# Threshold attention and an MLP on one core: ten blocks by products of quarters instead of eight, and the division of x^T moved to other engines

## The chip, the core and the metric

The kernel runs on one core of a Trainium2 chip. The core has five engines that run side by side, each through its own list of instructions in order: TensorE (PE, with its weight loads as PEld) multiplies matrices, VectorE (DVE) and ScalarE (ACT) work element by element, GpSimd (POOL) does the same more freely and issues transfers, and SyncE (SP) issues transfers. TensorE writes to PSUM, a small memory of banks; everything else is in SBUF. The metric is the time of one execution in microseconds on the device. The kernel before takes 1418.27 us, the median of three runs (1416.62 to 1419.5).

## The reference

q, k and v have 8 batches, 8 heads, 576 rows and 64 columns. They come in single precision, the weights w_in (512 x 2048) and w_out (2048 x 512) as doubles.

```
scores = scale * q @ k^T                         # per head, 576 x 576
thresh = max(scores, axis=-1) - tau
scores = where(scores >= thresh, scores, -1e9)
attn   = exp(scores - max(scores)) / (sum + 1e-09)
x      = attn @ v, the heads side by side        # 4608 x 512
h      = x @ w_in                                # 4608 x 2048
g      = 0.5 * h * (1 + erf(h / sqrt(2)))        # exact Gelu
out    = g @ w_out                               # 4608 x 512
```

## The kernel before

**Pairs, chunks and slots.** Two heads of a batch form a pair; there are 32 pairs, four to a batch. The 576 rows of a pair are worked on in five chunks: chunks 0 to 3 have 128 rows of each head, and chunk 4 has the last 64 rows of both heads together. A chunk is a slot of the main loop (L824), and the document names slots of a pair by the chunk, 0 to 4. The first four pairs (batch 0) are the early ones: their slots come in another order (two chunks of each pair, then three of each), since during them the weights are loaded and converted as well. The early part has 20 slots, the rest 140.

**A slot.** TensorE forms the scores of the chunk in two PSUM tiles, one a head (`scores`, L358; one tile in chunk 4). There are only two such tiles, so the scores of the next slot wait for the end of this slot's softmax. VectorE takes the negated maximum of each (`nmx`, L370), GpSimd derives the threshold (`thr`, L371), ScalarE the exponential (L373), VectorE multiplies it by the comparison with the threshold and sums (L389), and, beyond the early pairs, transposes the result in squares of 32 (`turn_p`, L436). SP moves the squares to their places in `pT` (`regroup`, L454, L458). In slot 2 of the next pair, `weigh_v` (L460) multiplies pT by V into two PSUM tiles of x^T. The softmax isn't divided by its sums before that; `divisors` (L405), in slot 4, takes the reciprocals and sends them through DRAM into a row on all partitions, `inv`. After `weigh_v`, VectorE multiplies x^T by `inv` out of PSUM into the block `x_blk` in SBUF (L492), in pieces that end at blocks of 256 tokens. For the early pairs the division is made earlier, and ScalarE copies x^T (L490).

**The MLP.** Tokens are taken in 18 blocks of 256. `block_steps` (L538) gives a plain block: 64 matmuls of 256 columns into hT (L549), Gelu by ScalarE (L522), and 32 matmuls of 512 columns into o_ps (L563), a copy and a store. ScalarE has the Gelu and the exponential in different tables; `table` (L532) brings the exponential's back with a dummy. In the early part hT is only copied, and its Gelus wait in a list, `held`, until slot 20. `fill` issues matmuls of plain blocks between the scores of one slot and the next. How many it issues is a plan written by hand: `GOAL` says how many blocks are to be done by which slot, `goal` draws lines between, and `PARTS` spreads a pair's share over its five slots. The plan doesn't look at the time that anything takes. `tokens` says up to which token the blocks may be taken.

**Products of quarters.** The last 8 blocks (`PLAIN = N_BLK - 8`) aren't worked on during the attention. They wait as x in SBUF, three of them (`AWAY`) in DRAM (`put_away`, `bring`), and `strassen` (L654) does them two at a time, a duo, with seven products of quarters instead of eight in both layers, at the price of sums on VectorE. `weights_in` (L612) forms the sums of w_in after the last chunk.

**The start.** `load_early` brings q and k of an early pair: q by SP's queue, k by ScalarE's for pairs 0 and 1, else by SP's. `load_piece` brings a piece of the weights twice, as it is and shifted by a byte (L156, L158), on GpSimd's queue, and `convert` lets VectorE and ScalarE turn pieces to single precision (L178 to L188) for a given number of nanoseconds in each slot. GpSimd clears `q_tail` and `v_sb` first of all, and tau is the first thing on SP's queue.

Of the kernel before, what the change touches and what calls it, by code (L numbers as in the profile page):

```python
# [18 lines left out]
def kernel(  # L19
# [46 lines left out]
    TOK = 256  # L66
    N_BLK = B * S // TOK
    PLAIN = N_BLK - 8

    AWAY = [PLAIN, PLAIN + 1, PLAIN + 2]  # L70
    order = list(range(PLAIN + 3, N_BLK)) + AWAY
# [33 lines left out]
    for t in q_tail + v_sb:  # L105
        nc.gpsimd.memset(t, 0.0)
# [4 lines left out]
    tau_sb = const.tile([P, 1], FP32, name="tau_sb")  # L111
    nc.sync.dma_start(tau_sb, tau[0].partition_broadcast(P))
    some = const.tile([P, 1], FP32, name="some")
    nc.vector.tensor_scalar(some, tau_sb, 0.0, None, op0=ALU.is_ge)
    q_scale = const.tile([P, 1], FP32, name="q_scale")
    nc.vector.tensor_scalar(q_scale, some, SCALE, None, op0=ALU.mult)
    lift = const.tile([P, 1], FP32, name="lift")
    nc.vector.tensor_scalar(lift, some, -ALL, ALL, op0=ALU.mult, op1=ALU.add)
    tau_eff = const.tile([P, 1], FP32, name="tau_eff")
    nc.vector.tensor_scalar(tau_eff, tau_sb, lift, None, op0=ALU.max)  # L120
# [18 lines left out]
    def load_piece():  # L139
        if loaded[0] == len(pieces):  # L140
            return
        dst, src = pieces[loaded[0]]
        loaded[0] += 1
        if not wide:
            nc.sync.dma_start(dst, src)
            converted[0] += 1
            load_piece()
            return
        k = loaded[0] - 1
        if k % 2:  # L150

            room = pd[k // 2 % 2].bitcast(U32)
            raw, shifted = room[:, 0:2 * PIECE], room[:, 2 * PIECE:4 * PIECE]
        else:
            raw, shifted = (xg.tile([P, 2 * PIECE], U32, tag="x", name=s) for s in ("raw", "shifted"))
        nc.gpsimd.dma_start(raw, src.bitcast(U32))  # L156
        n = 8 * PIECE - 4
        nc.gpsimd.dma_start(shifted.bitcast(U8)[:, 0:n], src.bitcast(U8)[:, 3:3 + n])  # L158
        raws.append((dst, raw, shifted))
# [300 lines left out]
    def weigh_v(p, lo, hi):  # L460
# [34 lines left out]
        if by is not None:  # L495
            return divide
        divide()
# [289 lines left out]
    load_early(0)  # L787
    nc.scalar.activation(warm[:, 1:2], warm[:, 0:1], AF.Exp)
    load_early(1)
    for _ in range(2):  # L790
        load_piece()
# [25 lines left out]
    PARTS = 1.2, 1.2, 0.8, 1.2, 0.6  # L817
# [6 lines left out]
    for n in range(len(slots) + WEIGH + 1):  # L824
# [12 lines left out]
        made = []  # L837
# [3 lines left out]
        if p > EARLY and i == WEIGH:  # L841
            made = [weigh_v(p - 1, lo, hi) for lo, hi in ((0, WIDE), (WIDE, S))]
# [45 lines left out]
        convert(3000 if n < 2 * HP else 3650 if n < BATCH - 1 else 1e9)  # L888
# [15 lines left out]
        elif p > EARLY and i == WEIGH and p % HP == 0:  # L904
# [38 lines left out]
```

## Time and profile before

| what | value |
|---|---|
| median of three runs | 1418.27 us |
| the profiled execution | 1413.93 us |
| its span | 1412.1 us |
| early part, to the first maximum of slot 20 | 0 to 152.1 us |
| first matmul by quarters (chain) | 1019.11 us |
| VectorE: maxima L370, products L389, transposes L436 | 749, 816, 1376 ns each |
| ScalarE: exponential L373, table load L522, Gelu L522 | 738, 1283, 597 ns each |
| VectorE: multiplies of x^T, L492 | 104 of them, 31.7 us |
| GpSimd: thr L371 | 292 ns each |

The profile is of one execution, 0.3% below the median. A row of the page gives an engine's operation with its line, what it writes and reads, how often, its total and mean time, and the idle time before it. The granted clock of TensorE was 0.997 in this execution. TensorE's busy time takes modelled ends for its matmuls, so it says less than the times between starts. One float32 matmul shows as two records. In the timeline, one row can stand for several instructions of a group that follow each other, and its duration then reaches from the first start to the last end.

### The profile page before, as it was taken

The numbers are of one execution on the slowest core, as the hardware profiler recorded it, in microseconds if no ns is written. First come the engines' busy times: TensorE is split into PE (matmuls) and PEld (weight loads), VectorE is DVE, ScalarE is ACT, GpSimd is POOL, SyncE is SP. The second block draws the span as 40 slices with busy tenths as digits, with TensorE's granted clock in tenths as the row PEclk, the third lists the DMA queues.
The fourth block names the chain that finished last, engine by engine and source line by source line (L and its number), as shares of the span: only waits on it lengthen the run. The fifth ranks groups of instructions, "written<-read, shape, count | busy, mean of one in ns | idle before, by whom it ended". The sixth has DMA issues, their size and how long they took to land.

```text
span 1412.1 us, 19647 instructions
## 1 busy us (share of the span) xinstructions
PE 1377.0 (98%) x6544; PEld 956.6 (68%) x6544; DVE 886.8 (63%) x1772; ACT 636.3 (45%) x1052; POOL 389.0 (28%) x812
## 2 busy tenths in 40 slices
PE   6899899999999999999999999999999999999999
PEld 4677557466475564655746657466588888888887
DVE  5888687777777777777777777777664142241330
ACT  5766628445255373563745627447141140230320
POOL 4444244343344344344334344330000000000000
PEclk9999999999999999999999999999999999999999
DMA  9979267666666766666766776664400000001000
GB/s 259 294 276 261 68 140 154 134 150 127 141 150 135 162 131 140 143 146 150 164 132 145 164 158 143 148 140 100 108 1 8 23 1 26 19 1 51 9 8 23
DMA packets 219346, 167.05 MB, mean 118 GB/s; under 512 B 122480, under 2 KB 203952, under 8 KB 219248
## 3 DMA queue, kind: packets, MB, share of 16 engines
q1 hardware_dynamic: 193040, 108.65, 36.5%
q0 software_dynamic: 23808, 56.57, 13.1%
q8 instruction: 53, 0.87, 0.3%
q10 hardware_dynamic: 2400, 0.59, 0.2%
q14 instruction: 45, 0.37, 0.1%
HBM read 71.68 MB, written 11.47 MB: 59 GB/s over the span
## 4 chain that ended last, share of the span: by engine, by line
PE 91%; DVE 4%; ACT 3%; DMA 2%; issue 1%; SPq 0%; POOL 0%; DVEq 0%; ACTq 0%; POOLq 0%
PE bank L683 27%; PE hT L549 20%; PE o_ps L563 19%; PE sc L358 12%; PE xT L475 10%; PE tr L301 2%; DVE p L389 1%; ACT p L373 1%; DMA q<-in_q_dram 1%; DVE power L186 1%; DMA turned_p<-in_moe_w_in_dram 1%; DVE nmx L370 0%; DVE w_in L188 0%; ACT diag L403 0%; DVE power L178 0%
## 5 line engine op out<-in xcount | busy, mean ns | idle before, releaser
L373 ACT ACTIVATE p<-sc,nmx 128x576 f32<-128x576 f32 x288 | 202.1, 738 | 370.8 <-DVE nmx L370 370.6
L370 DVE TENSOR_REDUCE nmx<-sc 128x1 f32<-128x576 f32 x288 | 205.1, 749 | 163.1 <-PE sc L358 163.0
L563 PE MATMUL o_ps<-w_out,g 128*128 128x512 f32 x640 | 294.3, 602 | 3.0 <-ACT g L522 3.0
L549 PE MATMUL hT<-x,w_in 128*128 128x256 f32 x1280 | 296.1, 384 | 0.0
L549 PEld LDWEIGHTS hT<-x,w_in 128*128 128x128 f32 x1280 | 238.6, 190 | 56.0 <-issue 25.1
L389 DVE SCALAR_TENSOR_TENSOR p<-sc,thr,p 128x576 f32<-128x576 f32 x288 | 225.4, 816 | 65.1 <-ACT p L373 62.7
L371 POOL TENSOR_SCALAR thr<-nmx,tau_eff 128x1 f32<-128x1 f32 x288 | 84.1, 292 | 541.8 <-DVE nmx L370 541.8
L563 PEld LDWEIGHTS o_ps<-w_out,g 128*128 128x128 f32 x640 | 116.5, 190 | 142.6 <-issue 137.8
L358 PE MATMUL sc<-kT,qT 64*128 64x288 f32 x960 | 165.1, 437 | 1.4 <-DVE p L389 1.0
L475 PE MATMUL xT<-pT,v 128*64 128x256 f32 (+1 forms) x1280 | 163.7, 409 | 2.7 <-ACT g L522 2.7
L436 DVE STREAM_TRANSPOSE turned_p<-p 128x1152 f32<-128x1152 f32 x112 | 154.1, 1376 | 2.9
L358 PEld LDWEIGHTS sc<-kT,qT 64*128 64x128 f32 x960 | 93.4, 190 | 82.9 <-issue 70.3
L475 PEld LDWEIGHTS xT<-pT,v 128*64 128x64 f32 x1280 | 89.8, 137 | 74.0 <-issue 10.8
L233 POOL DMA_DIRECT2D v<-in_v_dram x208 | 110.5, 534 | 10.7 <-issue 9.8
L683 PE MATMUL bank<-x,w_in 128*128 128x256 f32 x384 | 93.3, 379 | 0.0
L683 PE MATMUL bank<-w_out,unit 128*128 128x256 f32 x416 | 92.4, 379 | 0.0
L522 ACT ACT_TABLE_LOAD x67 | 86.0, 1283 | 1.2
L535 ACT ACT_TABLE_LOAD x67 | 86.0, 1283 | 1.2
L683 PEld LDWEIGHTS bank<-w_out,unit 128*128 128x128 f32 x416 | 79.1, 190 | 10.7
L683 PEld LDWEIGHTS bank<-x,w_in 128*128 128x128 f32 x384 | 73.0, 190 | 10.3 <-issue 0.5
L224 POOL DMA_DIRECT2D q<-in_q_dram x104 | 70.7, 685 | 16.0 <-issue 15.1
L224 POOL DMA_DIRECT2D k<-in_k_dram x104 | 69.6, 675 | 0.7 <-DMA inv<-turned 0.3
(152 smaller groups left out, 1307.3 us busy)
## 6 DMA issues: line engine op xcount, KB each, us to landing
pT<-turned_p SPq DMA_DIRECT2D x448, 160.0 KB, 3.5
pT<-pd_tail SPq DMA_DIRECT2D x112, 80.0 KB, 2.9
q<-in_q_dram POOLq DMA_DIRECT2D x104, 72.0 KB, 4.1
k<-in_k_dram POOLq DMA_DIRECT2D x104, 72.0 KB, 2.6
inv<-turned SPq DMA_DIRECT2D x56, 128.0 KB, 3.9
v<-in_v_dram POOLq DMA_DIRECT2D x156, 40.0 KB, 3.2
out_dram<-o_sb SPq DMA_DIRECT2D x20, 256.0 KB, 4.3
raw<-in_moe_w_in_dram POOLq DMA_DIRECT2D x8, 512.0 KB, 5.6
```

What stands on the lines that cost most here:

```text
L224: eng.dma_start(t[e * D + f:e * D + f + Q], rows[:, :, f:f + Q])
L233: eng.dma_start(t[r:P:4, e, 0:n, :], rows[:, r * KR:r * KR + n, :])
L358: nc.tensor.matmul(sc[e][:, h, 0:HALF], lhsT=lhsT, rhs=s["kT"][rows, at:at + HALF], start=True, stop=True)
L370: nc.vector.tensor_reduce(nmx[:, e:e + 1], sc, axis=AXIS.XY, op=ALU.max, negate=True)
L373: nc.scalar.activation(w[:, e * S:(e + 1) * S].rearrange("p (h s) -> p h s", h=2), sc, AF.Exp, bias=nmx[:, e:e + 1], scale=1.0)
L389: nc.vector.scalar_tensor_tensor(row, sc[e][:, :, 0:HALF], thr[:, e:e + 1], row, op0=ALU.is_ge, op1=ALU.mult, accum_out=den[e])
L436: nc.vector.transpose(turned_p[:, :, i // 2, 0:NB, i % 2 * Q:(i % 2 + 1) * Q], w.rearrange("p (e b i) -> p e b i", e=2, i=Q))
L475: nc.tensor.matmul(to, lhsT=s["v"][:, e, c, :], rhs=rhs, start=(c == 0), stop=(c == KR - 1))
L522: nc.scalar.activation(t, src, AF.Gelu)
L549: nc.tensor.matmul(hT[:, j % 2, :], lhsT=w_in_sb[c][:, j * P:(j + 1) * P], rhs=x_blk[n][:, c, :], start=(c == 0), stop=(c == N_DM - 1))
L563: nc.tensor.matmul(o[:, 0:d_model], lhsT=g[j][:, m * P:(m + 1) * P], rhs=w_out_sb[j], start=(j == 0), stop=(j == N_DF - 1))
L683: nc.tensor.matmul(to, lhsT=l, rhs=r, start=start and k == 0, stop=k == len(pairs) - 1, skip_group_check=not start)
```

## The change

Four things are changed. Ten blocks instead of eight go by quarters (`PLAIN = N_BLK - 10`), five of them by way of DRAM. x^T beyond the early pairs is copied out of PSUM by ScalarE, as it was for the early ones, and multiplied by `inv` in SBUF by GpSimd, a pair at a time (`divide`), in slot 3 (`DIVIDE`), after that slot's thr; for the last pair in the slot of its weighing. A batch's tokens are let into the MLP one slot later. `GOAL` and `PARTS` have other numbers. At the start, k of pair 1 comes on GpSimd's queue ahead of the memsets, tau behind the q of pair 0, the first two pieces of weights on SP's queue; slot 0 has no conversion, and slots 1 to 7 have 3400 ns instead of 3000.

```diff
-    PLAIN = N_BLK - 8
-
-    AWAY = [PLAIN, PLAIN + 1, PLAIN + 2]
-    order = list(range(PLAIN + 3, N_BLK)) + AWAY
+    PLAIN = N_BLK - 10
+
+    AWAY = list(range(PLAIN, PLAIN + 5))
+    order = list(range(PLAIN + 5, N_BLK)) + AWAY
...
-    for t in q_tail + v_sb:
-        nc.gpsimd.memset(t, 0.0)
...
-    tau_sb = const.tile([P, 1], FP32, name="tau_sb")
-    nc.sync.dma_start(tau_sb, tau[0].partition_broadcast(P))
...
-    def load_piece():
+    def load_piece(eng=nc.gpsimd):
...
-        nc.gpsimd.dma_start(raw, src.bitcast(U32))
+        eng.dma_start(raw, src.bitcast(U32))
...
-        nc.gpsimd.dma_start(shifted.bitcast(U8)[:, 0:n], src.bitcast(U8)[:, 3:3 + n])
+        eng.dma_start(shifted.bitcast(U8)[:, 0:n], src.bitcast(U8)[:, 3:3 + n])
...
-            eng = nc.scalar if p < 2 and name == "k" else nc.sync
+            eng = (nc.scalar, nc.gpsimd)[p] if p < 2 and name == "k" else nc.sync
...
-        by = None if p < EARLY else s["inv"]
-        if hi == S:
-            del st[p]
-
-        def divide():
-            at = lo
-            while at < hi:
-                n, o = divmod(b * S + at, TOK)
-                size = min(TOK - o, hi - at)
-                if n not in x_blk:
-                    x_blk[n] = xg.tile([P, N_DM, TOK], FP32, tag="x", name="x")
-                to, x = x_blk[n][:, hp, o:o + size], xT[:, at - lo:at - lo + size]
-                if by is None:
-                    nc.scalar.copy(to, x)
-                else:
-                    nc.vector.tensor_tensor(to, x, by[:, at:at + size], op=ALU.mult)
-                at += size
...
+        for n, o, at, size in in_blocks(b, lo, hi):
+            if n not in x_blk:
+                x_blk[n] = xg.tile([P, N_DM, TOK], FP32, tag="x", name="x")
+            nc.scalar.copy(x_blk[n][:, hp, o:o + size], xT[:, at - lo:at - lo + size])
+
+    def in_blocks(b, lo, hi):
+        while lo < hi:
+            n, o = divmod(b * S + lo, TOK)
+            size = min(TOK - o, hi - lo)
+            yield n, o, lo, size
+            lo += size
+
+    def divide(p):
+        b, hp = divmod(p, HP)
+        by = st.pop(p)["inv"]
+        for n, o, at, size in in_blocks(b, 0, S):
+            x = x_blk[n][:, hp, o:o + size]
+            nc.gpsimd.tensor_tensor(x, x, by[:, at:at + size], op=ALU.mult)
...
     load_early(0)
+    tau_sb = const.tile([P, 1], FP32, name="tau_sb")
+    nc.sync.dma_start(tau_sb, tau[0].partition_broadcast(P))
...
     load_early(1)
+    for t in q_tail + v_sb:
+        nc.gpsimd.memset(t, 0.0)
     for _ in range(2):
-        load_piece()
+        load_piece(nc.sync)
...
+    DIVIDE = 3
...
-    GOAL = [(-1, 0.0), (START - 1, 0.0), (BATCH - 1, 0.5)]
-    GOAL += [(BATCH * (m + 2) + WEIGH, x) for m, x in enumerate([1.96, 3.3, 4.64, 5.98, 7.32, 8.66, PLAIN])]
+    GOAL = [(-1, 0.0), (START - 1, 0.0), (BATCH - 1, 0.42)]
+    GOAL += [(BATCH * (m + 2) + DIVIDE, x) for m, x in enumerate([1.96, 2.97, 3.98, 4.98, 5.99, 6.99])]
+    GOAL += [(BATCH * B + WEIGH, PLAIN)]
...
-    PARTS = 1.2, 1.2, 0.8, 1.2, 0.6
+    PARTS = 1.3, 1.3, 0.2, 1.3, 0.9
...
         if p > EARLY and i == WEIGH:
-            made = [weigh_v(p - 1, lo, hi) for lo, hi in ((0, WIDE), (WIDE, S))]
+            for lo, hi in (0, WIDE), (WIDE, S):
+                weigh_v(p - 1, lo, hi)
+            if p == NP:
+                divide(p - 1)
...
-        if made:
-            made[0]()
...
-        if made:
-            made[1]()
...
+        if EARLY < p < NP and i == DIVIDE:
+            divide(p - 1)
...
-        convert(3000 if n < 2 * HP else 3650 if n < BATCH - 1 else 1e9)
+        convert(0 if n == 0 else 3400 if n < 2 * HP else 3650 if n < BATCH - 1 else 1e9)
...
-        elif p > EARLY and i == WEIGH and p % HP == 0:
+        elif p > EARLY and i == DIVIDE and p % HP == 0 or p == NP and i == WEIGH:
             tokens = p // HP * S
```

More of the change, by code (lines that the diff above doesn't have):

```diff
@@ L104 @@
     pd_tail = [const.tile([P, 4 * KR, Q], FP32, name=f"pd_tail{i}") for i in range(2)]
-    for t in q_tail + v_sb:
-        nc.gpsimd.memset(t, 0.0)
-    tau_sb = const.tile([P, 1], FP32, name="tau_sb")
-    nc.sync.dma_start(tau_sb, tau[0].partition_broadcast(P))
-    some = const.tile([P, 1], FP32, name="some")
-    nc.vector.tensor_scalar(some, tau_sb, 0.0, None, op0=ALU.is_ge)
     q_scale = const.tile([P, 1], FP32, name="q_scale")
-    nc.vector.tensor_scalar(q_scale, some, SCALE, None, op0=ALU.mult)
-    lift = const.tile([P, 1], FP32, name="lift")
-    nc.vector.tensor_scalar(lift, some, -ALL, ALL, op0=ALU.mult, op1=ALU.add)
     tau_eff = const.tile([P, 1], FP32, name="tau_eff")
-    nc.vector.tensor_scalar(tau_eff, tau_sb, lift, None, op0=ALU.max)
     rebias = const.tile([P, 1], FP32, name="rebias")
@@ L476, in weigh_v @@
                     to, lhsT=s["v"][:, e, c, :], rhs=rhs, start=(c == 0), stop=(c == KR - 1))
-        by = None if p < EARLY else s["inv"]
-        if hi == S:
-            del st[p]
-        def divide():
-            at = lo
-            while at < hi:
-                n, o = divmod(b * S + at, TOK)
-                size = min(TOK - o, hi - at)
-                if n not in x_blk:
-                    x_blk[n] = xg.tile([P, N_DM, TOK], FP32, tag="x", name="x")
-                to, x = x_blk[n][:, hp, o:o + size], xT[:, at - lo:at - lo + size]
-                if by is None:
-                    nc.scalar.copy(to, x)
-                else:
-                    nc.vector.tensor_tensor(to, x, by[:, at:at + size], op=ALU.mult)
-                at += size
-        if by is not None:
-            return divide
-        divide()
+        for n, o, at, size in in_blocks(b, lo, hi):
[14 more added lines that the diff above has]
+            nc.gpsimd.tensor_tensor(x, x, by[:, at:at + size], op=ALU.mult)
     NS_IN, NS_OUT = 4 * TOK / 2.4, 4 * d_model / 2.4
@@ L787 @@
     load_early(0)
+    tau_sb = const.tile([P, 1], FP32, name="tau_sb")
+    nc.sync.dma_start(tau_sb, tau[0].partition_broadcast(P))
+    some = const.tile([P, 1], FP32, name="some")
+    nc.vector.tensor_scalar(some, tau_sb, 0.0, None, op0=ALU.is_ge)
+    nc.vector.tensor_scalar(q_scale, some, SCALE, None, op0=ALU.mult)
+    lift = const.tile([P, 1], FP32, name="lift")
+    nc.vector.tensor_scalar(lift, some, -ALL, ALL, op0=ALU.mult, op1=ALU.add)
+    nc.vector.tensor_scalar(tau_eff, tau_sb, lift, None, op0=ALU.max)
     nc.scalar.activation(warm[:, 1:2], warm[:, 0:1], AF.Exp)
     load_early(1)
+    for t in q_tail + v_sb:
+        nc.gpsimd.memset(t, 0.0)
     for _ in range(2):
-        load_piece()
+        load_piece(nc.sync)
     turn_qk_early(0)
@@ L836 @@
         table()
-        made = []
         for args in due:
```

## The prediction

> **What bounds the kernel now.** I read the page first, its busy times and slices:
>
> ```profile
> PE 1377.0 (98%) x6544; PEld 956.6 (68%) x6544; DVE 886.8 (63%) x1772; ACT 636.3 (45%) x1052; POOL 389.0 (28%) x812
> ```
>
> TensorE is busy in nearly all of the span, but its ends are modelled, so the length of work has to come from runs without a break. The chain that ended last, in order of time, gives such runs at the end of the attention and after it (start, duration, what):
>
> ```profile
> 1001.03 9.44 PE o_ps L563 x22
> 1010.48 5.00 PE xT L475 x40
> ...
> 1067.10 96.98 PE bank L683 x448
> ...
> 1164.58 96.97 PE bank L683 x448
> ```
>
> 22 records of the second layer take 9.44, so 0.429 each; a run of 10 hT records in the same chain takes 2.16, so 0.216. A matmul is two records. A plain block of 256 tokens is 64 hT and 32 o_ps matmuls: 128 x 0.216 + 64 x 0.429 = 55.1 us. A duo by quarters takes 97.48 (1067.10 to 1164.58) where two plain blocks take 110.2.
>
> From 20 slots on, TensorE sets the pace of the attention too. The weighing of V starts once in a pair; in the chain, 20 pairs lie between 285.37 and 894.35, so 30.45 us a pair. The work: 1.34 blocks in four pairs, 18.46 us a pair; xT 5.00; scores 4 x 1.17 + 0.98 = 5.66. The sum is 29.1; 1.3 is left for changes between groups of matmuls and for waits. Where the wait is, the chain shows around a last chunk (i = 4):
>
> ```profile
> 631.58 4.49 PE o_ps L563 x10
> 636.07 0.98 PE sc L358 x4
> ...
> 637.08 0.77 DVE nmx L370
> ...
> 637.87 0.75 ACT p L373
> ...
> 638.71 0.83 DVE p L389 x2
> ...
> 639.68 1.21 PE sc L358 x6
> ```
>
> The last chunk has one head-sized tile, so its softmax runs with nothing to overlap: 3.61 us from its scores to where the next chunk's second tile may be written. TensorE fills that with 0.98 of scores and only 4 to 5 o_ps or hT matmuls (1.72 to 2.16 us), so it waits 0.3 to 0.7.
>
> The other slots, by the timeline (start, duration, engine):
>
> ```profile
> 599.44 1.24 PE L358 MATMUL sc<-kT,qT 64*128 64x288 f32 x8
> 600.61 4.58 PE L549 MATMUL hT<-x,w_in 128*128 128x256 f32 x20
> 600.71 1.42 DVE L370 TENSOR_REDUCE nmx<-sc 128x1 f32<-128x576 f32 x2 [2.21 <-PE sc L358]
> 601.50 1.41 ACT L373 ACTIVATE p<-sc,nmx 128x576 f32<-128x576 f32 x2 [4.41 <-DVE nmx L370]
> ...
> 602.23 0.29 POOL L371 TENSOR_SCALAR thr<-nmx,tau_eff 128x1 f32<-128x1 f32 x1 [0.29 <-DVE nmx L370]
> ...
> 602.72 2.14 POOL L233 DMA_DIRECT2D v<-in_v_dram  x4 [0.21 <-issue]
> 602.92 1.28 ACT L522 ACT_TABLE_LOAD   x1
> ...
> 603.94 1.38 DVE L436 STREAM_TRANSPOSE turned_p<-p 128x1152 f32<-128x1152 f32 x1
> ```
>
> VectorE waits 2.21 us for scores: it has slack. From the scores' start the last masked product ends 4.46 later (603.90) and the transpose 5.88 later; VectorE's own cycle is 1.42 + 0.21 + 1.56 + 1.42 = 4.61. ScalarE's cycle, where a slot has a Gelu, is 1.41 of exponentials, two table loads of 1.28, Gelu 0.60 and the dummy exponential 0.20: 4.8.
>
> Last, the start, where TensorE is not the bound:
>
> ```profile
> 16.34 1.08 PE L275 MATMUL tr<-ident,k 128*128 128x128 f32 x4 [3.78 <-DMA q<-in_q_dram]
> ...
> 19.80 0.69 DVE L186 SCALAR_TENSOR_TENSOR power<-raw,power 128x512 uint32<-128x512 uint32 x1 [4.37 <-ACT power L179]
> ...
> 21.89 1.40 DVE L370 TENSOR_REDUCE nmx<-sc 128x1 f32<-128x576 f32 x2
> ```
>
> The second pair's keys come late, ScalarE waits in its order for them, and VectorE stands 4.37 us behind ScalarE.
>
> **What the Trainium skill says.** ScalarE: Activation LUTs, "What ACT_TABLE_LOAD costs" gives 1283 ns a load plus a drain of about 1380; the trace has the 1283 (L522), but the Gelu starts 1.30 after its load does, so I add no drain. The same page, "Table sets: the hidden batching unit", says copies are in every set, so the x^T copies on ScalarE bring no loads; L490 in the early pairs agrees (0.375 for 256 columns, no load before it). SBUF — State Buffer, "SBUF: two separate sides", lets GpSimd and VectorE shut each other out for a whole instruction when VectorE reads two tensors from SBUF. In the attention its large operations read PSUM and one SBUF tensor, or one tensor; no run here shows such a block. DMA: Bandwidth & Descriptors, "Issuing engines are not separate DMA queues": moving issues saves issue time, not bandwidth; the trace, with 0.9 to 1.1 of the engines busy from 0 to 60 us, has no case against it.
>
> **The change, part by part.**
> *Two blocks more by quarters.* TensorE loses 110.2 and gains 97.5: -12.7 us if it stays the bound. Two more blocks go out to DRAM and back (512 KB, 4.7 us to land): the way back is hidden behind the 48 us of a duo's second half, as for L649 before, which waited up to 5.5 without TensorE stopping; the way out is behind four or more slots and ScalarE needs the room at the next weighing, so uncovered it would cost a few us once for each of five blocks.
>
> *Slots.* The plan now gives 1.01 blocks in four pairs: 13.9 us a pair. By PARTS and the order in which the matmuls are issued, slots 0, 1 and 3 get 3.44 to 3.88, slot 2 0.4 to 0.9, slot 4 mostly 2.58. With 1.17 of scores and some 0.2 between groups, slots 0, 1, 3 take 4.8 to 5.2, slot 2 (with xT) 6.9, slot 4 3.6. VectorE needs 4.61 in 0, 1, 3; slot 2 adds 1.73 of transposes, 6.35, the divide gone; slot 4 3.75. So TensorE keeps the lead, by 0.2 to 0.5 us a slot where it was 1.2. In slot 4 the wait of 0.3 to 0.7 nearly closes (0.98 + 2.58 against 3.61): -0.4 x 28 = -11. A pair becomes 13.9 + 5.0 + 5.66 + 0.9 = 25.5.
>
> *Cost of thin cover.* ScalarE in a pair with Gelus in each slot: 4 x 4.8 + 4.1 (slot 4) + 0.76 (scaling q) + 1.1 (four copies of some 0.28) = 25.2 against 25.5. It runs late by 0.5 after slot 4 and 0.8 after slot 1, and catches up in slot 2, where TensorE is 2.5 us away. Behind a late table load stand the exponentials of the next chunk, behind them its masked products, and behind these TensorE's next scores. I take 0.2 to 0.3 for each of some 14 such pairs, +4; with no loss 0, with each late piece passed on +15.
>
> *Divide on GpSimd.* VectorE loses 104 multiplies (31.7 us). GpSimd gets three multiplies a pair, in slot 3, behind both thr and ahead of four V loads (2.14) that stand ahead of slot 4's thr. No run shows such a multiply. GPSIMD Engine Reference, "Elementwise — side-by-side cycle accounting", has 4497 ns for 2048 fp32: 576 columns make 1.27 us as an estimate; with nothing for each start 1.3 is the low end, with the 0.29 of a one-column thr for each it is 2.1. I take 1.7. GpSimd is free at 3.08 + 0.4 + 1.7 + 2.1 = 7.3 after slot 3's scores; slot 4's exponential ends at about 7.8. So thr with 0.29 is in time up to 2.1: cost 0. Beyond, each us is a us on the 3.61 chain, 28 times. It also waits for the divisors' row, whose last transfer left at 619.27 and lands in 4.0, in slot 2, and for ScalarE's copies, done in slot 2; the next divisors, written to the same single buffer, leave only after slot 4. The MLP may touch a finished batch from slot 4 on, and the plan is then a fraction of a block short of needing it. Behind these waits on GpSimd stand only the V loads, for a pair that is two ahead, and thr.
>
> *The seam to the quarters.* After the last chunk VectorE needs 13.2 us for sums of weights and blocks (1004.82 to 1018.03). TensorE's second product needs them and came at about 1019.8. Now TensorE has 2.6 + 3 x 2.9 + 5.0 + 1.0 of cover, 1.5 less than before, against 1.8 to spare and 0.9 of divides that are gone: 0.
>
> *Start.* Keys of pair two come on GpSimd's queue, three issues of some 0.6, ahead of its 3 us of memsets (which then end at about 6, before q_tail is written at 9.20), weight pieces behind q on SP's; V of pair one, needed at 34 us, goes later by their four issues (2.4). Scores two can start when product one frees PSUM, at about 14, so maxima at 16.5, not 21.89. But 3.5 us of conversion done meanwhile are now owed (0 in slot 0, 3400 for 3000 after): about -2, from 0 to -4. The early plan drops from 0.5 to 0.42 blocks: 4.4 us of TensorE work leave slots 10 to 19, where it is busy 40 of 40 us, and are in the later sum: the -105.8 there and the -4.4 here make the 110.2. I count 1 us less because VectorE (33 of 40) follows closely. Fewer held Gelus at slot 20: -1.
>
> Sum: -12.7 + 1 - 11 + 4 - 2 - 1 = -21.7. The profiled execution took 1413.9 (span 1412.1, 1.8 around it), 4.3 below the median 1418.27. I take 3 off the gain for terms that I can't see: about 1395 profiled, 1399 as a median.
>
> **Rivals.**
> (A, 0.68) As worked out, -11 to -29: 1389 to 1407, most likely 1399.
> (B, 0.20) The two-block gain stays, but ScalarE's late exponentials eat the rest: +15 instead of +4 and no gain in slot 4. -12.7 + 1 + 15 - 3 - 1 is about 0 at the worst, and half of that lateness gives -8: 1407 to 1419. For it: 25.2 of 25.5. Against: slot 2's slack.
> (C, 0.12) GpSimd is slower than thought: at 3.2 us a pair thr comes 1.1 late, 28 x 1.1 = +31: 1430. It decides from about 2.9 (28 x 0.8 = 22 eats the gain). For it: an unseen operation, and spans there are rough; against: the estimate can grow by 70% before that.
> (D, inside A and B) The keys come early but the weights' transfers then set the start: 0 for -2.
>
> **How the numbers follow.** Two executions of this kernel differ by about 0.2%, 2.8 us, which is the bound of "same". The range 1389 to 1415 holds nine tenths of A and most of B: 0.8. Faster: A and four fifths of B, 0.84. Same: the end of B, 0.04. Slower: C, 0.12.
>
> **What would show it.** Right: five runs of 97 us of bank records; pairs of 25.4 to 26 us; TensorE unbroken; maxima two at 16 to 17 us; multiplies on GpSimd under 2.1 a pair; VectorE waiting for scores still, but tenths. Wrong: VectorE's product waiting for thr in slot 4 (C); exponentials waiting for ScalarE's own table loads and scores for products (B); pairs above 26.5; ScalarE's copies waiting for the way out to DRAM.

## The result, and the profile after

The changed kernel takes 1394.61 us (median of four runs, 1394.05 to 1395.27), the kernel before 1417.44 in the four runs beside it (1414.52 to 1419.5). The ratio is 0.9841, with an interval of 0.9822 to 0.9859: faster by 22.8 us. Forecast were 1399 and a range of 1389 to 1415. The profiled execution took 1395.27 us, its span is 1393.5.

The page of the changed kernel, its busy times and two of its rows (the idle time ahead of an operation stands at the end of a row):

```profile
PE 1360.1 (98%) x6608; PEld 967.6 (69%) x6608; DVE 891.4 (64%) x1734; ACT 640.4 (46%) x1165; POOL 433.4 (31%) x895
...
L379 DVE SCALAR_TENSOR_TENSOR p<-sc,thr,p 128x576 f32<-128x576 f32 x288 | 225.4, 816 | 70.0 <-ACT p L363 68.9
L360 DVE TENSOR_REDUCE nmx<-sc 128x1 f32<-128x576 f32 x288 | 205.3, 750 | 69.4 <-PE sc L348 68.6
```

The same two operations in the kernel before:

```profile
L370 DVE TENSOR_REDUCE nmx<-sc 128x1 f32<-128x576 f32 x288 | 205.1, 749 | 163.1 <-PE sc L358 163.0
L389 DVE SCALAR_TENSOR_TENSOR p<-sc,thr,p 128x576 f32<-128x576 f32 x288 | 225.4, 816 | 65.1 <-ACT p L373 62.7
```

TensorE stays the busiest. VectorE's idle time ahead of its maxima, where it waits for scores, falls from 163.1 to 69.4: more than half of the slack that it had is used up. Its wait for exponentials ahead of the masked products has hardly grown (62.7 to 68.9), and the threshold from GpSimd has no place in the row.

The chain of the changed kernel around a last chunk, and at the end (start, duration, what):

```profile
521.92 4.08 PE hT L536 x18
526.00 0.97 PE sc L348 x4
526.97 2.59 PE hT L536 x12
529.56 1.26 PE sc L348 x8
```

```profile
900.27 2.77 PE o_ps L550 x6
903.04 47.50 PE bank L670 x220
...
951.04 96.97 PE bank L670 x448
...
1048.52 96.97 PE bank L670 x448
```

In the piece of the chain before that the prediction shows, the chain left TensorE after the scores of the last chunk and ran through maximum, exponential and masked product. Here 2.59 us of hT fill that place and the chain stays on TensorE. At the end there are five duos; 951.04 to 1048.52 is 97.48 us for one. The first maximum of slot 159 (the last chunk) came at 1001.07 before and comes at 885.46, the first matmul by quarters at 1018.95 and 902.88: 116.1 us earlier. One more duo costs 97.5, and 116.1 - 97.5 is the 18.6 by which the spans of the two profiled executions differ. That this is 4 less than the medians say is taken up below.

By the starts of the first maxima in each slot, from slot 40 on (23 pairs), a pair takes 25.66 us where it took 30.45. Slots 0 to 4 take 5.04, 4.96, 6.92, 4.93 and 3.81; before it was 5.92, 5.87, 9.39, 5.52 and 3.75. Slot 4 isn't shorter, it has more of the MLP in it.

What TensorE waits after a last chunk can hide inside a row of the chain. The second head's scores in the next pair's slot 0 need the PSUM tile that the last chunk's softmax still holds, and a wait for it only makes the row of the eight score records longer. In the changed kernel:

```profile
400.15 1.30 PE hT L536 x6
401.44 1.88 PE sc L348 x8
```

Without a wait such a row lasts 1.17. In slots 1 to 3 the starts of a slot's eight score records lie within 0.84 us, in all 23 pairs before and after. In slot 0 they lie within 1.27 on average before and 1.04 in the changed kernel: the wait falls from 0.43 to 0.20 us a pair, and isn't gone. The experiments below give this number as the wait in the first scores.

The same place in the timeline of the changed kernel, with GpSimd's new work (start, duration, engine):

```profile
522.92 0.29 POOL L361 TENSOR_SCALAR thr<-nmx,tau_eff 128x1 f32<-128x1 f32 x1 [3.33 <-DVE nmx L360]
...
523.75 1.70 POOL L484 TENSOR_TENSOR x<-x,inv 128x256 f32<-128x256 f32 x3
...
525.39 2.16 POOL L223 DMA_DIRECT2D v<-in_v_dram  x4
...
527.80 0.74 ACT L363 ACTIVATE p<-sc,nmx 128x576 f32<-128x576 f32 x1 [3.62 <-DVE nmx L360]
527.95 0.30 POOL L361 TENSOR_SCALAR thr<-nmx,tau_eff 128x1 f32<-128x1 f32 x1 [0.40 <-DVE nmx L360]
...
528.64 0.82 DVE L379 SCALAR_TENSOR_TENSOR p<-sc,thr,p 128x576 f32<-128x576 f32 x1 [0.88 <-ACT p L363]
```

Three multiplies take 1.70 us, the issues of V stand behind them until 527.55, and thr of slot 4 is done at 528.25, before the exponential (528.54). The masked product waits for the exponential, not for GpSimd.

The start, on VectorE in the changed kernel:

```profile
14.84 1.42 DVE L360 TENSOR_REDUCE nmx<-sc 128x1 f32<-128x576 f32 x2 [0.41 <-PE sc L348]
...
21.89 1.40 DVE L360 TENSOR_REDUCE nmx<-sc 128x1 f32<-128x576 f32 x2
...
32.28 0.43 DVE L168 TENSOR_SCALAR power<-raw 128x512 uint32<-128x512 uint32 x1 [4.61 <-DMA raw<-in_moe_w_in_dram]
```

Here slots are numbered through the early part, from 0. The maxima of slot 1 (pair 0's second chunk, whose scores stand on TensorE behind the turning of pair 1's keys) start at 14.84 instead of 21.89, those of slot 2, pair 1's first, at 21.89 instead of 29.16. Then VectorE stands 4.61 us in front of a piece of the weights that hasn't landed, and of the 7.3 us of lead 3.0 are left in slot 3 (32.70 against 35.65) and 0.5 in slot 6 (56.16 against 56.65).

### The profile page after: what moved, and what is told of

Its sections match the earlier page's. It is cut to its first block, busy times and chain, and to the rows that moved or that the text cites. A ratio compares the mean times of both kernels' runs of the same rounds, so it can differ in the third digit from the quotient of the medians.

```text
span 1393.5 us, 19980 instructions
## 1 busy us (share of the span) xinstructions
PE 1360.1 (98%) x6608; PEld 967.6 (69%) x6608; DVE 891.4 (64%) x1734; ACT 640.4 (46%) x1165; POOL 433.4 (31%) x895
## 4 chain that ended last, share of the span: by engine, by line
PE 88%; DVE 5%; DMA 3%; ACT 3%; issue 1%; SPq 0%; POOL 0%; ACTq 0%; DVEq 0%
PE bank L670 35%; PE o_ps L550 16%; PE hT L536 14%; PE sc L348 12%; PE xT L465 10%; DVE p L379 1%; DVE power L176 1%; ACT p L363 1%; DMA k<-in_k_dram 1%; ACT diag L393 1%; DVE power L168 1%; DVE w_in L178 1%; DMA turned_p<-in_moe_w_in_dram 1%; DMA turned_p<-in_moe_w_out_dram 1%; DVE w_out L178 1%
## 5 line engine op out<-in xcount | busy, mean ns | idle before, releaser
L379 DVE SCALAR_TENSOR_TENSOR p<-sc,thr,p 128x576 f32<-128x576 f32 x288 | 225.4, 816 | 70.0 <-ACT p L363 68.9
L360 DVE TENSOR_REDUCE nmx<-sc 128x1 f32<-128x576 f32 x288 | 205.3, 750 | 69.4 <-PE sc L348 68.6
L536 PE MATMUL hT<-x,w_in 128*128 128x256 f32 x1024 | 241.1, 385 | 0.0
L550 PE MATMUL o_ps<-w_out,g 128*128 128x512 f32 x512 | 237.3, 604 | 2.1 <-ACT pT L302 2.1
L536 PEld LDWEIGHTS hT<-x,w_in 128*128 128x128 f32 x1024 | 189.5, 190 | 49.2 <-issue 23.5
L550 PEld LDWEIGHTS o_ps<-w_out,g 128*128 128x128 f32 x512 | 92.9, 189 | 112.7 <-issue 108.6
L670 PE MATMUL bank<-x,w_in 128*128 128x256 f32 x480 | 116.7, 379 | 0.0
L670 PE MATMUL bank<-w_out,unit 128*128 128x256 f32 x520 | 115.5, 379 | 0.0
L670 PEld LDWEIGHTS bank<-w_out,unit 128*128 128x128 f32 x520 | 98.8, 190 | 13.4
L670 PEld LDWEIGHTS bank<-x,w_in 128*128 128x128 f32 x480 | 91.2, 190 | 12.8 <-issue 0.5
L670 PE MATMUL bank<-v,unit 128*128 128x256 f32 x320 | 82.1, 379 | 0.0
L670 PE MATMUL bank<-unit,turned_p 128*128 128x256 f32 x320 | 73.1, 379 | 0.0
```

The costliest lines, as they stand in the source:

```text
L360: nc.vector.tensor_reduce(nmx[:, e:e + 1], sc, axis=AXIS.XY, op=ALU.max, negate=True)
L379: nc.vector.scalar_tensor_tensor(row, sc[e][:, :, 0:HALF], thr[:, e:e + 1], row, op0=ALU.is_ge, op1=ALU.mult, accum_out=den[e])
L536: nc.tensor.matmul(hT[:, j % 2, :], lhsT=w_in_sb[c][:, j * P:(j + 1) * P], rhs=x_blk[n][:, c, :], start=(c == 0), stop=(c == N_DM - 1))
L550: nc.tensor.matmul(o[:, 0:d_model], lhsT=g[j][:, m * P:(m + 1) * P], rhs=w_out_sb[j], start=(j == 0), stop=(j == N_DF - 1))
L670: nc.tensor.matmul(to, lhsT=l, rhs=r, start=start and k == 0, stop=k == len(pairs) - 1, skip_group_check=not start)
```

## The experiments

Each is the changed kernel with the edit shown. The kernel before ran beside them, with medians of 1415.8 to 1416.9, where it had 1417.44 beside the changed kernel; so a difference of 1 to 2 us between two experiments isn't clear of noise. Pairs, slots and waits are taken as above, from slot 40 on.

**What the two new blocks and the new shares are worth.** Eight blocks by quarters, with the goals and the shares of before:

```diff
-    PLAIN = N_BLK - 10
+    PLAIN = N_BLK - 8
...
-    PARTS = 1.3, 1.3, 0.2, 1.3, 0.9
+    PARTS = 1.2, 1.2, 0.8, 1.2, 0.6
```

(`AWAY` and `order` are those of before too, and `GOAL` has the numbers of before.)

> Eight blocks by quarters as before, with the goals and shares of the kernel before; x^T by ScalarE and GpSimd and the new start are kept. Theory (TensorE was the bound, VectorE's relief alone frees no time that it can use): the slots 0, 1 and 3 keep their length, some 0.2 us of slot 2 or 4 may close, pairs of 30.2 to 30.5 us against 30.45, and 1412 to 1417 us. Rival (the multiplies on VectorE themselves held up the pairs): 28 pairs times the 1.1 us that left VectorE, part of it at least, so pairs below 29.8 us and 1385 to 1403.

1416.65 us (1414.39 to 1419.0), ratio 1.0006 (0.9998 to 1.0013), pairs of 30.47. The relief of VectorE and the new start, with the old plan, bring nothing that can be measured. The theory holds. The wait in the first scores is 0.43 us a pair, as in the kernel before. The chain of this run around a last chunk:

```profile
604.29 0.97 PE sc L348 x4
605.27 2.16 PE hT L536 x10
607.42 1.69 PE sc L348 x8
```

The same with the new shares, so that only `PARTS` differs from the run above:

> Eight blocks by quarters with the goals of the kernel before, but the new shares; x^T by ScalarE and GpSimd and the new start are kept. Theory (the term of -11 for the wait in slot 4 doesn't need fewer blocks): slots 0, 1 and 3 at about 6.2 us, slot 2 at 7.1 to 7.4, slot 4 at 4.5: pairs of 30.0 to 30.2 us against 30.47 with the old shares, 1403 to 1411 us. Rival (the wait went only because less work is left in the pairs): pairs as with the old shares, 1413 to 1419 us.

1406.99 us (1406.44 to 1407.53), ratio 0.9934 (0.9919 to 0.995): 9.7 less than with the old shares. Slots 0 to 4 take 6.21, 6.18, 7.32, 5.94 and 4.44, pairs 30.09. The chain of this run around a last chunk:

```profile
622.66 1.17 PE sc L348 x8
623.83 4.49 PE o_ps L550 x10
628.32 0.97 PE sc L348 x4
629.29 3.43 PE o_ps L550 x8
632.73 1.17 PE sc L348 x8
```

3.43 us of o_ps cover the softmax of the last chunk's tile, and the next scores take 1.17 where they took 1.69. Both chains stay on TensorE here; only the longer row tells them apart. The wait in the first scores falls from 0.43 to 0.01 us a pair, with as many blocks in the attention, and 28 x 0.42 is 11.8 of which 9.7 are measured. From here to the changed kernel the two blocks are missing, with their goals: 1406.99 - 1394.61 = 12.4.

**The shares, the other way.** With ten blocks by quarters, all the shares of before:

```diff
-    PARTS = 1.3, 1.3, 0.2, 1.3, 0.9
+    PARTS = 1.2, 1.2, 0.8, 1.2, 0.6
```

> The changed kernel with the shares of the kernel before (PARTS 1.2, 1.2, 0.8, 1.2, 0.6). Theory: slot 4 gets 1.7 us of MLP instead of 2.6 under its chain of 3.6 us, so TensorE waits some 0.9 us more in a pair, and slots 0, 1 and 3 fall below VectorE's 4.6 now and then: 25 to 30 us slower, 1420 to 1425. Rival, the same work is only moved between slots of a pair: 0 to 3 us.

1420.87 us (1419.63 to 1424.77), ratio 1.0035 (1.0024 to 1.0047): the two blocks are worth nothing without the shares. Slot 2 has 8.74 us, slots 0, 1 and 3 have 4.89, 4.77 and 4.74, slot 4 has 3.78. The wait in the first scores is 1.24 us a pair. The time is as expected, but the run changes five shares at once. So slot 4 alone:

```diff
-    PARTS = 1.3, 1.3, 0.2, 1.3, 0.9
+    PARTS = 1.3, 1.3, 0.5, 1.3, 0.6
```

> 0.3 of a share, 0.83 us of the plan's matmuls, goes from slot 4 back to slot 2 (1.3, 1.3, 0.5, 1.3, 0.6); slots 0, 1 and 3 are as changed. Theory of the prediction (slot 4 can't be shorter than the softmax of its one tile, so TensorE waits there for whatever it isn't given): slot 4 stays at 3.75 and slot 2 grows from 6.9 to 7.6 or 7.8, 28 x 0.6 to 0.8 more, 1410 to 1417 us. Rival (slot 4 has no such wait, the shares matter for VectorE in slots 0, 1 and 3): slot 4 shortens by what slot 2 gains, 1393 to 1398 us.

1421.09 us (1418.62 to 1422.69), ratio 1.0028 (1.0015 to 1.0041). Slot 4 keeps 3.76, slot 2 grows to 7.77: the rival is out, a matmul taken from slot 4 isn't saved there. But the loss of 26.5 lies above what was expected. The wait in the first scores is 1.16 us a pair, 0.96 more than in the changed kernel, and 28 x 0.96 is 26.9: the loss is this wait. The next pair's scores begin 2.62 us after those of the last chunk instead of 3.63, so the edit took 1.0 us of matmuls from slot 4 where 0.83 were meant. In one pair the chain of this run goes over ScalarE:

```profile
534.24 1.22 PE sc L348 x8
535.46 0.75 DVE nmx L360
...
536.23 1.41 ACT p L363 x2
...
537.66 1.28 ACT L509
...
538.95 0.60 ACT g L509
...
539.57 1.28 ACT L522
...
541.07 0.64 ACT p L363
```

A Gelu with its two table loads (L509, L522) stands in front of the last chunk's exponential: ScalarE's late exponential, the mechanism of rival B. But it is late by 0.1 us only. The last chunk's masked product starts 2.81 us after the chunk's scores at the earliest; its lateness beyond that, summed over the 23 pairs, is 1.7 us here and 1.1 in the changed kernel. So this is a small part of the loss.

**Whether TensorE is still the bound.** Twelve blocks by quarters, seven by way of DRAM:

```diff
-    PLAIN = N_BLK - 10
+    PLAIN = N_BLK - 12
...
-    AWAY = list(range(PLAIN, PLAIN + 5))
+    AWAY = list(range(PLAIN, PLAIN + 7))
...
-    GOAL += [(BATCH * (m + 2) + DIVIDE, x) for m, x in enumerate([1.96, 2.97, 3.98, 4.98, 5.99, 6.99])]
+    GOAL += [(BATCH * (m + 2) + DIVIDE, x) for m, x in enumerate([1.96, 2.63, 3.3, 3.98, 4.65, 5.33])]
```

> Twelve blocks by quarters (seven by way of DRAM), everything else as changed, with the goals scaled to what is left. Theory (with ten blocks the bound of TensorE is used up: VectorE needs 3 x 4.61 + 6.35 + 3.75 = 23.9 us a pair, and with the delays seen in slots 0 to 3 some 24.5): pairs fall only from 25.66 to 24.2 to 25, so 28 x 0.7 to 1.5 is gained where 97.5 is paid for one more duo: 1445 to 1475 us. Rival (TensorE is still the bound in all slots): another -12.7, 1382 us; pairs of 21.7 us.

1467.39 us (1465.74 to 1468.91), ratio 1.0364 (1.0346 to 1.0382). Pairs of 24.71, with slots 0, 1 and 3 at 4.75, 4.61 and 4.60, which is VectorE's own cycle of 4.61. TensorE now waits in the scores of slots 0, 1 and 2, 1.61, 0.52 and 0.61 us a pair. The chain of this run goes round by the other engines:

```profile
534.69 1.22 PE sc L348 x8
535.91 0.76 DVE nmx L360
...
536.69 0.75 ACT p L363
...
538.28 0.83 DVE p L379 x3
...
539.13 1.38 DVE turned_p L426
...
543.84 3.38 DMA pT<-turned_p
```

With these shares ten blocks are about where TensorE and VectorE meet in these slots: one duo more costs 97.5 at the end and frees 28 x 0.95. Shares made for twelve blocks weren't tried.

**GpSimd's multiply.** Doubled, so that x^T is multiplied by `inv` twice and the output isn't the attention's:

```diff
-            nc.gpsimd.tensor_tensor(x, x, by[:, at:at + size], op=ALU.mult)
+            for _ in range(2):
+                nc.gpsimd.tensor_tensor(x, x, by[:, at:at + size], op=ALU.mult)
```

> The changed kernel with each multiply by the divisors on GpSimd issued twice (x^T is multiplied by them twice, so the values of x change), 3.4 us a pair instead of 1.7. Theory: GpSimd is free for slot 4's threshold at about 9.0 us after slot 3's scores, the exponential of slot 4 ends at about 7.8 and the threshold takes 0.3, so the masked product of slot 4 comes 1.4 us late, TensorE waits for it, and 28 pairs lose some 30 to 40 us: 1425 to 1435. VectorE's products would show a wait for thr. Rival, the lateness is made up elsewhere: under 5 us.

1430.27 us (1427.73 to 1433.02), ratio 1.0102. Slot 4 takes 5.19 us, the others stay. VectorE's masked products, among the groups of this run:

```profile
L379 DVE SCALAR_TENSOR_TENSOR p<-sc,thr,p 128x576 f32<-128x576 f32 x288 | 225.4, 816 | 100.1 <-POOL thr L361 52.2 <-ACT p L363 42.2 <-ACT g L510 5.4
```

Now they wait for thr, 52.2 us in all. Six multiplies take 3.71 us where three took 1.70, so GpSimd has 2.01 more to do, and a pair grows by 1.42: some 0.6 of room were left behind its multiplies. This is rival C, made by hand.

**The division back on VectorE**, out of PSUM in slot 2 as before, with everything else as changed (ScalarE's copies stay for the early pairs only, `divide` isn't called, and the calls of `finish` stand where they stood before; these lines aren't shown):

```diff
-            nc.scalar.copy(x_blk[n][:, hp, o:o + size], xT[:, at - lo:at - lo + size])
+            if p < EARLY:
+                nc.scalar.copy(x_blk[n][:, hp, o:o + size], xT[:, at - lo:at - lo + size])
+
+        def finish():
+            by = s["inv"]
+            for n, o, at, size in in_blocks(b, lo, hi):
+                nc.vector.tensor_tensor(
+                    x_blk[n][:, hp, o:o + size], xT[:, at - lo:at - lo + size], by[:, at:at + size], op=ALU.mult)
+        return finish
```

> The changed kernel with the multiply by the divisors again on VectorE, out of PSUM, in slot 2, all else as changed. Theory: VectorE needs 4 x 4.6 + 1.75 + 1.13 more in slot 2 and 3.75 in slot 4, some 25.1 us a pair where TensorE sets 25.5, and in slot 2 7.5 to 7.6 where TensorE has 6.9, so 0.3 to 0.6 us a pair are lost: 28 x that is 8 to 17 us, 1403 to 1412. Rival, slots 3 and 4 make it up and the move of the multiply was worth nothing: 1394 to 1397.

1424.31 us (1418.41 to 1429.09), ratio 1.0061: 30 more than changed, where 8 to 17 were expected. Slot 2 takes 8.56 where 6.92 were. The multiplies in this run, by their size (the last figure of each row is the idle time by its cause):

```profile
L476 DVE TENSOR_TENSOR x<-xT,inv 128x192 f32<-128x192 f32 x28 | 9.6, 344 | 11.1 <-DMA inv<-turned 8.9 <-PE xT L465 2.2
L476 DVE TENSOR_TENSOR x<-xT,inv 128x128 f32<-128x128 f32 x32 | 8.4, 281 | 7.6 <-DMA inv<-turned 6.1 <-issue 0.9
L476 DVE TENSOR_TENSOR x<-xT,inv 128x256 f32<-128x256 f32 x20 | 8.2, 413 | 8.8 <-DMA inv<-turned 7.0 <-issue 1.6
L476 DVE TENSOR_TENSOR x<-xT,inv 128x64 f32<-128x64 f32 x24 | 5.0, 206 | 2.3 <-DMA inv<-turned 1.9 <-issue 0.5
```

The rows add up to 31.2 us; where multiplies overlap, their time is in two of them, and together they keep VectorE busy for 28.0. They wait 23.9 for the divisors' row. In the kernel before these multiplies (L492: 31.7 by rows, 28.4 together) waited 6.4 us for everything, and not for the row. The row goes out in slot 4 and comes back through DRAM; the pair got 4.8 us shorter with the change, the way of the row did not, so a consumer in slot 2 that had it in time before now stands in front of it. That was missing in the expectation. To part the two causes, VectorE does the multiply in SBUF in slot 3, when the row has landed, after ScalarE's copy:

```diff
-            nc.gpsimd.tensor_tensor(x, x, by[:, at:at + size], op=ALU.mult)
+            nc.vector.tensor_tensor(x, x, by[:, at:at + size], op=ALU.mult)
```

> The multiply of x^T in SBUF is done by VectorE instead of GpSimd, at the same place, slot 3, when the divisors' row has long landed; ScalarE still copies x^T out of PSUM. Theory (VectorE's time is what counts: 1.1 us more in a slot where it has 0.3 to 0.5 us of slack): slot 3 grows by 0.6 to 1 us, pairs of 26.3 to 26.7, 1411 to 1424 us. Rival (in the run with the divide on VectorE in slot 2 only the wait for the divisors' row mattered): pairs stay under 25.9 us, 1394 to 1401 us.

1406.05 us (1402.19 to 1407.79), ratio 0.9927, between the two. VectorE never waits for the row here; its 84 multiplies, 23.9 us together, make slot 3 5.47 instead of 4.93, pairs 26.16. Of 0.85 us a pair 0.5 come through: slot 3 had 0.3 to 0.4 of room, and the theory had the multiply at 1.1. Both expectations miss the time, and both causes are real: VectorE's time alone costs 11 us in slot 3, and the wait for the row is in the trace of the run with slot 2. How the other 19 of the 30 us divide between that wait and the place of the multiplies in slot 2, these runs don't show. GpSimd in slot 3 escapes both: its multiplies wait for the row once, 16.4 us at the last pair.

**ScalarE under the thin cover.** Every copy of x^T beyond the early pairs twice:

```diff
-            nc.scalar.copy(x_blk[n][:, hp, o:o + size], xT[:, at - lo:at - lo + size])
+            for _ in range(1 if p < EARLY else 2):
+                nc.scalar.copy(x_blk[n][:, hp, o:o + size], xT[:, at - lo:at - lo + size])
```

> ScalarE makes every copy of x^T beyond the early pairs twice, 1.1 us a pair more in slot 2. Theory of the prediction (ScalarE is the engine behind the thin cover: 25.2 us of work in a pair with a Gelu in each slot, and it catches up only in slot 2): in the 14 pairs with three or four Gelus it now has 26.3 us, so these grow by 0.4 to 0.8 us, the others by nothing: 1399 to 1408 us. Rival (the thin cover costs nothing, ScalarE has room in slot 2): all pairs keep their length, 1393 to 1397 us.

1395.14 us (1393.66 to 1397.15), ratio 0.9855 (0.9836 to 0.9875): 0.5 more than changed, within what executions differ by. The pair with the most Gelus, as busy times of each engine in its window, first of the changed kernel, then of this one:

```profile
530.76:556.53 25.77, 25.77 (x138) 17.46 (x137) 21.92 (x41) 21.19 (x31) 13.79 (x28) 1.00 0.74 166
```

```profile
527.49:553.26 25.77, 25.77 (x138) 17.46 (x137) 21.90 (x41) 22.19 (x35) 13.79 (x28) 1.00 0.74 166
```

After the window and its length stand PE, PEld, DVE, ACT and POOL. ScalarE (ACT) goes from 21.19 to 22.19, and the pair stays at 25.77. The wait in the first scores is 0.20 us a pair in both runs. In 22 of the 23 pairs nothing moves; in one ScalarE's doubled copies, late behind a wait, add 1.3 us. The theory falls.

**The start undone.** k of pair 1, tau, the memsets, the first pieces of weights and the conversion's budget as before:

> The changed kernel with the start of the kernel before (k of pair 1 on ScalarE's queue, memsets and tau first, weight pieces on GpSimd's queue, 3000 ns of conversion in each of the first eight slots). Theory: the lead of 7.3 us that the early keys give at slot 2 is lost by slot 6 to waits for the weights and for VectorE's owed conversions (0.5 us are left in the trace), so undoing it costs 0 to 2.5 us: 1394.6 to 1397. Rival, the lead carries and something else took it back in the trace: 5 to 7 us slower, 1400 to 1402.

The lines of tau and the memsets, which go back too, are left out here:

```diff
-        load_piece(nc.sync)
+        load_piece()
...
-            eng = (nc.scalar, nc.gpsimd)[p] if p < 2 and name == "k" else nc.sync
+            eng = nc.scalar if p < 2 and name == "k" else nc.sync
...
-        convert(0 if n == 0 else 3400 if n < 2 * HP else 3650 if n < BATCH - 1 else 1e9)
+        convert(3000 if n < 2 * HP else 3650 if n < BATCH - 1 else 1e9)
```

1396.04 us (1395.56 to 1397.21), ratio 0.9855 (0.9836 to 0.9874). The start is worth 1.4 us by the medians, within the 0 to 2.5 expected, but the interval of the ratio overlaps that of the changed kernel, so a worth of nothing isn't ruled out. Maxima of slot 2 come at 28.8 again, 6.9 later than changed. Those of slot 20 come 1.1 later (150.67 against 149.60), which says nothing: nine profiles with the changed kernel's early part have them between 147.89 and 153.27.

**A better version.** In slot 20 of the changed kernel the plan finishes hT and begins with o_ps at once:

```profile
151.68 4.58 PE L536 MATMUL hT<-x,w_in 128*128 128x256 f32 x20
...
153.09 3.23 ACT L509 ACTIVATE g<-g 128x512 f32<-128x512 f32 x6
...
158.41 1.63 PE L550 MATMUL o_ps<-w_out,g 128*128 128x512 f32 x2 [2.14 <-ACT pT L302]
...
162.29 1.42 DVE L360 TENSOR_REDUCE nmx<-sc 128x1 f32<-128x576 f32 x2 [8.09 <-PE sc L348]
```

The o_ps stand in front of the next scores and can start only after ScalarE's copies of pT (L302), which stand behind the held Gelus and a table load, and VectorE waits 8.09. The slot lasts 12.7 us. And once in the attention a copy of x^T waits for a block on its way out to DRAM:

```profile
625.35 0.27 ACT L470 COPY x<-xT 128x128 f32<-128x128 f32 x1 [2.32 <-DMA x<-x]
```

Its pair takes 26.37 us instead of some 25.3. So the plan is made to stop at the end of hT in slot 20, blocks may leave in slot 4 too, and 0.1 of a share goes from slot 2 to slot 4:

```diff
-    GOAL = [(-1, 0.0), (START - 1, 0.0), (BATCH - 1, 0.42)]
+    GOAL = [(-1, 0.0), (START - 1, 0.0), (BATCH - 1, 0.42), (BATCH, 0.478)]
...
-    PARTS = 1.3, 1.3, 0.2, 1.3, 0.9
+    PARTS = 1.3, 1.3, 0.1, 1.3, 1.0
...
-        elif leaving and i < 2:
+        elif leaving and (i < 2 or i == NC):
```

> An attempt at a better version: in slot 20 the plan stops after the last hT matmuls of the early layer, so that no o_ps stands in front of the held Gelus; blocks on their way to DRAM may leave in slot 4 too, so that none is still on its way when ScalarE's copies need the room; and 0.1 of a share moves from slot 2 to slot 4. Expected from the profile of the changed kernel: 1 to 3 us in slot 20, which lasts 12.7 us, about 1 us for the one wait on the way out, 0 to 1 for the share: 1390 to 1394 us. Rival: the work left out in slot 20 is only done later in the same slots, and the seam is set by the Gelus: 1394 to 1396.

1391.24 us (1389.77 to 1392.32), ratio 0.9826 (0.9809 to 0.9843): 3.4 faster than the changed kernel by the medians, 2 by the ratios, whose intervals overlap. The seam in this run:

```profile
152.81 4.58 PE L536 MATMUL hT<-x,w_in 128*128 128x256 f32 x20
...
157.32 1.24 PE L348 MATMUL sc<-kT,qT 64*128 64x288 f32 x8
```

The scores follow hT directly, slot 20 lasts 7.9 us, and slots 20 to 24 take 33.0 instead of 35.95. The changed kernel had TensorE's clock halved for 3.4 us there; two other runs with the same slots and no such stretch took 34.35 and 34.37, so 1.4 is the edit's. ScalarE's waits for the way out fall from 2.6 to 1.0, the wait in the first scores from 0.20 to 0.08 us a pair, pairs from 25.66 to 25.50.

## Why the prediction was right

**The two blocks, -12.7 and +1.** Right in size: 12.4 between the runs with eight and ten blocks, both with the new shares. A duo takes 97.48 as read from the profile before. The 12.4 isn't this term alone: it contains the wait that comes back with ten blocks (0.01 to 0.20 us a pair, 5 us), and the two profiles differ by 1.6 us at slot 20 and by 2.2 between the last chunk and the quarters.

**Slot 4, -11.** Right at eight blocks: 9.7 between the runs with old and new shares, and the wait of 0.43 us a pair is gone. In the changed kernel 0.20 of it is left, so there the term is 28 x 0.23 = 6. It is a separate gain, and the first is lost without it (1420.87 with the old shares).

**GpSimd's multiply at 1.7, threshold in time, 0.** Right: 1.70 for three, 1.69 to 1.71 in all 28 pairs, so the block between GpSimd and VectorE that the prediction weighed doesn't show in them. The GPSIMD Engine Reference of the Trainium skill, "Elementwise — side-by-side cycle accounting", gave the estimate of 1.27 without a start for each; by size the trace has 323 ns for 64 columns and 729 for 256, so 2.1 ns a column and some 0.19 a start, which is where the value between the two ends came from. The limit of 2.1 a pair is near. Its own terms give 1.9: a thr of 0.29 ahead of an exponential that ends at 7.8 leaves GpSimd until 7.5, and 3.08 + 0.4 + 2.1 of it is taken. With the multiplies at 3.71 the pair grew by 1.42, which puts the limit at about 2.3.

**The thin cover, +4.** The pair came out, its account did not: this step failed. Forecast were 25.5 and 4/28 more for ScalarE's late exponentials, 25.64; measured are 25.66, of which 0.20 (5.6 us in all) is the wait in the first scores. So the 25.5 is right, and there is a loss of the size said. But ScalarE isn't its cause. In 19 of the 23 pairs the last chunk's masked product starts 2.81 us after the chunk's scores, as early as in any pair. In two it starts 0.09 later, behind a table load, and in two 0.18 and 0.72 later, because the maximum before it came late. The wait is there because the matmuls of slot 4 end before the softmax does: in four pairs the next scores begin at 3.22 us, in most of the others at 3.64, and the second head's can't begin before 4.09. TensorE's busy time doesn't show it (485.11 of 485.27 us in the 19 pairs from 377.80 to 863.07), since the ends of matmuls are modelled.

The working had a Gelu in each of five slots, 25.2 us for ScalarE. But slot 2 has a share of 0.2, too little for hT enough for a Gelu: there are four in a pair at most, and ScalarE has at most 21.3. So rival B was given more than it deserved. That -11 and +4 together are near the measured 0.23 us a pair is luck: the first was too large for ten blocks, the second had another cause.

**The start, -2.** Right in size, 1.4, but not clear of noise. What is left of the lead speaks for D: the maxima come early, as forecast (14.84, where 16 to 17 was said), and then the transfers of the weights set the pace, with 4.61 us in one place; no run took those transfers away. The section "Issuing engines are not separate DMA queues" of the skill's page DMA: Bandwidth & Descriptors says that transfers issued by different engines share the same DMA engines. That fits: the last of pair 1's keys landed at 7.58 instead of 16.55, but the piece of weights that VectorE stands in front of, issued at 26.11 (26.09 before), landed at 32.26 instead of 30.88, with the DMA engines busy throughout (their share is 1.03 and 1.07 in the two stretches of 10 us from 20 on).

**Held Gelus, -1, and the seam.** Wrong: slot 20 got longer, not shorter (12.69 us, 10.43 before), 1.6 of it by a stretch of halved clock. The better version found 1.4 us in slots 20 to 24. The seam to the quarters at 0 fits: from the first maximum of slot 159 to the first matmul by quarters it takes 17.4 us, 17.9 before. The wait for the way out to DRAM, named as a sign of a wrong prediction, showed once, 2.3 us, and cost some 1 us.

**3 off for terms unseen, and 4.3 for the median.** The sum without the 3 is 1413.9 - 21.7 = 1392.2 for an execution like the profiled one, and 1396.5 as a median; measured is 1394.61. The 3 had no row behind it and made the forecast worse, so that the profiled execution came out at the 1395 forecast for it (1395.27) is luck. The 4.3 had a cause, though it wasn't known: the granted clock. The profiled execution of the kernel before had 0.997 on average, that of the changed kernel 0.993. In 60 executions of the kernel before the time goes with the clock by 0.89 us for each 0.001 (they scatter about that line by 1.0 us); at 0.994 it is 1416.5, at 0.997 1413.8. With that slope the changed kernel at 0.994 has 1394.0, so the change is worth 22.5 at one clock, and four thousandths are the 3.6 us that the two spans, 18.6 apart, don't show. The same correction makes the steps 10.8 (shares) and 10.6 (two blocks). It assumes that the slope of one kernel holds for the others and that an edit doesn't itself set the clock. For the start the second may not hold: with it 13.7 to 23.9 us before slot 20 are at half clock in nine profiles, without it 6.8 and 10.2 in two.

What is left open: how the rest of the better version's gain divides between its edits, and why the clock is halved more often in the changed start.

## What to carry to other kernels

When work leaves the engine that bounds a loop, the next bound is already there in some of its stages: list each engine's own cycle stage by stage, and give each stage as much of the filling work as its slowest other engine can cover, or the gain is lost in the stages that are left empty (26 us with the old shares here, more than the whole gain of 22.8). A loop that gets shorter makes every transfer with a fixed way through DRAM later in terms of stages, so look for the consumer that had it just in time. A wait of TensorE inside a group of matmuls shows neither in its busy time nor as a break in the chain: compare the starts of the group's records with those of a group that has no wait. And before two profiled executions are subtracted, look at their granted clocks.

## What was not expected of the hardware

The time of one kernel follows the mean granted clock of TensorE, from 1411.26 at 0.996 and 1411.7 at 0.998 to 1419.84 at 0.990. In the records the clock is halved for stretches of 3.4 us or twice that: 6.8 us in the profile before and 20.5 in that of the changed kernel, all in the first 165 us apart from the very end. Nine profiles share the changed kernel's early part. The three with 13.7 us at half clock before slot 20 reach it at 147.9 to 149.2, the four with 17.1 at 149.6 to 150.8, the one with 20.5 at 150.82, the one with 23.9 at 153.27. And slots 20 to 24 take 35.94 to 36.00 us in four profiles with one stretch of 3.4 us there, and 34.35 and 34.37 in two without: 1.6 us for 3.4 at half clock. A single profile can't show a difference of 2 us in the early part.

A float32 multiply of two tensors costs GpSimd 0.73 us for 256 columns and VectorE 0.41, the latter whether one of them lies in PSUM (0.413) or not (0.412).
